# The last output tile of a fused attention and FFN kernel, computed and stored in two column halves

## Chip, cores and metric

The kernel runs on one core of one Trainium2 chip. The metric is the device time of one execution in microseconds (us); the time given for a kernel is the median over several executions. Engine names in the profile: PE is the matrix engine, PEld its weight loads, DVE the vector engine, ACT the scalar engine, POOL the general engine, SP the engine that mostly issues transfers. A "q" behind a name (SPq, ACTq) marks an instruction that the engine's sequencer issues, such as a DMA.

## What is computed

The reference is dilated sliding-window attention with 8 batches, 8 heads, 576 positions and head size 64, followed by a multiplicative feed-forward network without any non-linearity:

```python
attn = softmax(where(mask, q @ k.T / 8, -1e9))   # per head; half of the heads dilated by 4
x = (attn @ v).transpose(0, 2, 1, 3).reshape(4608, 512)
out = ((x @ w1) * (x @ w2)) @ w3 @ w_out         # d_ff 1024, output 4608 x 512, float32
```

## The kernel before

The kernel fuses `w3 @ w_out` into one matrix `wf_sb` early on, so that the network is two "up" products, an elementwise gate and one "down" product. Attention works batch by batch; its result lies transposed in the tiles XT. The up products (line 553) work on units of 288 tokens and chunks of 128 of the hidden size; ACT copies the first of a pair out of PSUM (564), and DVE multiplies it by the second into the ring `gt` (569). The down product (line 580) takes 128 tokens at a time: eight matmuls, one for each 128 of the hidden size, add up into one PSUM bank of 512 columns. For all tiles but the last, `copy_y` copies the bank to an SBUF tile `osb` on ACT (line 591), and `store` issues the transfer of its rows to memory on SP (line 614), mostly in two DMAs, because the tokens of a residue class lie four rows apart in the output. `osb` has three buffers.

The order of the work is made by a small planner (the class Plan). Each step is given to it with an engine, an assumed duration, what it depends on, a priority and the PSUM banks it needs. The planner plays the steps through in time, always taking the ready step with the smallest priority number, and chooses a bank. The instructions are then emitted in the order of the planned starts, so that each engine has one fixed order. The semaphore waits between engines are put in by the framework from what each instruction reads and writes.

The 36 down steps are added by `downs(i)` (line 929), with rising priority numbers. The last one, i = 35, comes after all up products are done; TensorE then has nothing but the last three down tiles left. Its output is not handled by `copy_y` and `store` but by `finish` (line 594): ACT copies columns 0 to 255 (601), DVE columns 256 to 511 (602), ACT issues the store of the first half (603) and SP that of the second (604). All 128 rows of this tile are one DMA for each half.

Of the kernel before, what the change touches and what calls it, by code (L numbers as in the profile page):

```python
# [10 lines left out]
P = 128  # L11
BF16 = mybir.dt.bfloat16
F32 = mybir.dt.float32
U32 = mybir.dt.uint32
AL = mybir.AluOpType
ACT = mybir.ActivationFunctionType
# [11 lines left out]
RING = 1152  # L28
# [31 lines left out]
class Plan:  # L60
# [10 lines left out]
    def add(self, name, eng, dur, deps, fn, prio, slot=0, lat=150, after=()):  # L71
        t = Task(name, eng, dur, deps, fn, prio + SHIFT.get(name, 0), slot, lat, after)
        self.tasks.append(t)
        return t
# [105 lines left out]
def kernel(  # L180
# [11 lines left out]
    nc = tc.nc  # L192
    B, H, s_, d_ = q.shape
    assert (s_, d_) == (S, D) and H == 8
    d_model = H * D
# [3 lines left out]
    KFF = d_ff // P  # L199
# [8 lines left out]
    wk_pool = ctx.enter_context(tc.tile_pool(name="wk", bufs=2))  # L208
# [7 lines left out]
    wf_sb = const.tile([P, KFF, d_model], BF16, name="wf_sb")  # L216
# [4 lines left out]
    gt = const.tile([P, KFF, RING], BF16, name="gt")  # L221
# [10 lines left out]
    def bank(n, dtype=F32):  # L232
        at = ps[:, plan.now.place or 0, :]
        return (at if dtype == F32 else at.bitcast(dtype))[:, 0:n]
# [306 lines left out]
    held = {}  # L541
# [34 lines left out]
    def down(i):  # L576
        y = bank(d_model)
        c0 = (i * P) % RING
        for f in range(KFF):
            nc.tensor.matmul(  # L580
                out=y,
                lhsT=gt[:, f, c0 : c0 + P],
                rhs=wf_sb[:, f, :],
                start=(f == 0),
                stop=(f == KFF - 1),
            )
        held[("y", i)] = y

    def copy_y(i):
        o_sb = wk_pool.tile([P, d_model], F32, tag="osb", bufs=3, name="osb")  # L590
        nc.scalar.copy(out=o_sb, in_=held[("y", i)])  # L591
        held[("o", i)] = o_sb

    def finish(i):

        o_sb = wk_pool.tile([P, d_model], F32, tag="osb", bufs=3, name="osb")
        b, x = i * P // S, i * P % S
        row = b * S + 4 * (x % RUN) + RES[x // RUN]
        rows = out[row : row + 4 * (P - 1) + 1 : 4, :]
        lo, hi = slice(0, d_model // 2), slice(d_model // 2, d_model)  # L600
        nc.scalar.copy(out=o_sb[:, lo], in_=held[("y", i)][:, lo])
        nc.vector.tensor_copy(out=o_sb[:, hi], in_=held[("y", i)][:, hi])
        nc.scalar.dma_start(out=rows[:, lo], in_=o_sb[:, lo])
        nc.sync.dma_start(out=rows[:, hi], in_=o_sb[:, hi])

    def store(i):
        o_sb = held[("o", i)]
        c0, end = i * P, (i + 1) * P
        at = c0
        while at < end:  # L610
            n = min(end, (at // RUN + 1) * RUN) - at
            b, x = at // S, at % S
            row = b * S + 4 * (x % RUN) + RES[x // RUN]
            nc.sync.dma_start(
                out=out[row : row + 4 * (n - 1) + 1 : 4, :], in_=o_sb[at - c0 : at - c0 + n, :]
            )
            at += n
# [9 lines left out]
    def w3_keep(ft):  # L627
        w3T[ft] = wk_pool.tile([P, KFF, P], BF16, tag="w3T", bufs=3, name="w3T")
        nc.scalar.copy(out=w3T[ft], in_=held[("x3", ft)])  # L629
# [21 lines left out]
    add = plan.add  # L651
# [29 lines left out]
    c0 = add("const2", "DVE", 1400, [c1], constants, -98)  # L681
# [39 lines left out]
    for i, nm in enumerate(WHOLE):  # L721
        t = add(f"LF{nm}", "SP", 100, [], lambda nm=nm: load_whole(nm, rows_of[nm], 0), -9 + i,
                lat=4400 + 1350 * i)
# [29 lines left out]
    FUSED, w3m = [], []  # L753
    for ft in sorted(lw3):
        x = add(f"W3T{ft}", "PE", 450, [lw3[ft], idt], lambda f=ft: w3_back(f), RANK["W"], slot=1,
                after=w3m[-3:-2])
        y = add("W3C", "ACT", 1012, [x], lambda f=ft: w3_keep(f), RANK["C"], lat=100, after=w3m[-3:-2])
# [5 lines left out]
        name = f"W3D{ft}"  # L763
# [30 lines left out]
    for b in range(B):  # L794
# [9 lines left out]
        for u in range(2):  # L804
# [3 lines left out]
            for half in range(2):  # L808
# [5 lines left out]
                name = f"VK{b}.{u}.{half}"  # L814
# [5 lines left out]
        if b >= DIRECT_V:  # L820
            hal = add(f"HALO{b}", "DVE", 820, LV[b] + [c0], lambda b=b: halo_v(b), 10 * b + 2,
                      lat=80)
# [46 lines left out]
        while steps < 4 * B:  # L869
            bb, i = steps // 4, steps % 4  # L870
# [7 lines left out]
            n = f"{bb}.{i}"  # L878
# [5 lines left out]
            if (bb, i) == (0, 2) and LATE:  # L884
                for t in late:
# [3 lines left out]
                     after=[prev["x"][i]])  # L889
# [5 lines left out]
            if bb < TURNED:  # L895
                x = add("X" + n, "PE", 310, ns + [idt], st.back, bb - 99 + rank("X", bb), slot=1)
                name = f"K{n}"
# [9 lines left out]
    seq = 10  # L907
    G, Y, gates, stores, pairs = {}, {}, [], [], []
# [20 lines left out]
    def downs(i):  # L929
        nonlocal seq  # L930
        seq += 1
        ks = {i * P // UNIT, (i * P + P - 1) // UNIT}
        y = add(f"Y{i}", "PE", 1728, [G[(k, f)] for k in ks for f in range(KFF)] + FUSED,
                lambda: down(i), seq, slot=1)
        Y[i] = y
        if i == n_y - 1:
            add("FIN", "ACT", 400, [y], lambda: finish(i), -1, lat=100, after=stores[-3:-2])
            return
        cy = add("CY", "ACT", 585, [y], lambda: copy_y(i), -1, lat=100,
                 after=[stores[-3] if len(stores) > 2 else None])  # L940
        stores.append(add("ST", "SP", 300, [cy], lambda: store(i), 0, lat=3000))

    n_y = n_tok // P
    done = 0
    half = KFF // 2
    begin = [(k, f + h) for h in (0, half) for k in range(2) for f in range(half)]
    for k, f in begin + [(k, f) for k in range(2, 2 * B) for f in range(KFF)]:
        ups(k, f)
        if k > 1 and f % 3 == 1 and (done + 1) * P <= k * UNIT:
            downs(done)  # L950
            done += 1
    while done < n_y:
        downs(done)
        done += 1
# [42 lines left out]
```

## Time and profile before

| | |
|---|---|
| median of 6 runs | 256.37 us (256.05 to 256.83) |
| profiled execution, its own time | 256.36 us |
| its span, first to last instruction | 254.6 us |
| granted TensorE clock, mean | 0.999 |
| HBM read, written | 38.80 MB, 9.44 MB |
| down matmuls L580, one | 379 ns |
| weight load for one (L580 PEld) | 98 ns |
| ACT copy of a whole tile (L591) | 586 ns |
| store on SP (L614), issue to landing, min/median/max | 1.6/2.6/7.8 us |

The span runs from the first to the last instruction that the hardware profiler recorded. A chain row gives a start, a length, the engine, the tile written and the source line; in the timeline, what stands in brackets is how long the engine was idle before the instruction and who released it. Matmuls are pipelined: the duration of one is a latency, and the distance between starts says how fast they go. A DMA's row is its issue only; its landing is a time of its own.

### The profile page before, as it was taken

Reading aid. Unit: us, or ns where it says so; the run is one execution under the profiler, and the core shown is the slowest. Engines: PE = TensorE matmul, PEld = TensorE weight load, DVE = VectorE, ACT = ScalarE, POOL = GpSimd, SP = SyncE. Lnnn points to the kernel's source line nnn. Section 1 sums busy time; section 2 is a strip of 40 time slices with the busy share of each in tenths; the row PEclk is TensorE's granted clock in tenths of the full one; section 3 lists DMA queues with packets and bytes.
Section 4 is the critical chain, followed back from the end, with each engine's and each line's share of the span. In section 5 each row is a group of like instructions: output and inputs, shape, how many; then the busy total and the mean of one; then the engine's idle time right before and its main releaser. Section 6 shows DMA issues by size and latency. Waiting matters only on the chain.

```text
span 254.6 us, 6758 instructions
## 1 busy us (share of the span) xinstructions
PE 244.5 (96%) x2723; PEld 169.3 (66%) x2755; DVE 165.3 (65%) x341; ACT 126.2 (50%) x221; POOL 66.4 (26%) x103
## 2 busy tenths in 40 slices
PE   7699999999999999999999999999999999999993
PEld 3488766565767666667676766676767667777661
DVE  3983447799889888678767877837737365333220
ACT  5677333986635534462626526355353543333331
POOL 7643129543522703008260310700000000000000
PEclk9999999999999999999999999999999999999999
DMA  7999999999999999829999667852232222311113
GB/s 225 208 199 206 206 211 211 207 99 181 189 146 182 206 187 170 185 67 147 162 162 144 89 78 103 136 84 64 67 65 67 66 68 73 99 41 44 41 41 124
DMA packets 59230, 33.40 MB, mean 131 GB/s; under 512 B 44736, under 2 KB 49088, under 8 KB 59200
## 3 DMA queue, kind: packets, MB, share of 16 engines
q0 software_dynamic: 38544, 18.81, 57.7%
q1 hardware_dynamic: 20512, 14.03, 24.2%
q8 instruction: 21, 0.34, 0.6%
q10 hardware_dynamic: 144, 0.13, 0.2%
q14 instruction: 9, 0.07, 0.1%
HBM read 38.80 MB, written 9.44 MB: 189 GB/s over the span
## 4 chain that ended last, share of the span: by engine, by line
PE 92%; ACT 3%; DMA 2%; DVE 1%; issue 1%; ACTq 0%
PE ps L553 50%; PE ps L580 24%; PE ps L634 5%; PE ps L481 4%; PE ps L445 4%; DMA gt<-in_q_dram 2%; ACT et L456 2%; PE ps L676 2%; PE ps L622 1%; PE ps L403 1%; PE ps L521 1%; ACT w3T L629 1%; DVE qt L394 1%; ACT qn L271 0%; DVE kt L379 0%
## 5 line engine op out<-in xcount | busy, mean ns | idle before, releaser
L553 PE MATMUL ps<-XT,w_sb 128*128 128x288 bf16 x1024 | 136.2, 286 | 0.0
L553 PEld LDWEIGHTS <-w_sb 128*128 128x128 bf16 x1024 | 97.8, 98 | 30.6
L569 DVE TENSOR_TENSOR gt<-ps,asb 128x288 bf16<-128x288 f32 x128 | 57.7, 455 | 52.0 <-PE ps L553 49.6
L564 ACT CAST asb<-ps 128x288 bf16<-128x288 f32 x128 | 50.9, 399 | 51.8 <-PE ps L553 49.5
L580 PE MATMUL ps<-wf_sb,gt 128*128 128x512 bf16 x260 | 65.9, 379 | 1.5
L591 ACT COPY osb<-ps 128x512 f32<-128x512 f32 x35 | 20.5, 586 | 56.3 <-PE ps L580 56.3
L580 PEld LDWEIGHTS <-gt 128*128 128x128 bf16 x288 | 28.2, 98 | 27.8
L293 POOL DMA_DIRECT2D vp<-in_v_dram x48 | 29.9, 630 | 43.1 <-PE ps L481 18.5
L456 ACT ACTIVATE et<-ps 128x1920 bf16<-128x1920 f32 (+2 forms) x21 | 34.2, 1634 | 5.5 <-PE ps L445 4.9
L504 DVE TENSOR_TENSOR xo<-ps,rcp 96x384 bf16<-96x384 f32 (+1 forms) x48 | 31.5, 675 | 0.6
L464 DVE TENSOR_TENSOR et<-et,mask 128x960 bf16<-128x960 bf16 (+1 forms) x34 | 21.4, 646 | 4.9 <-ACT et L456 4.7
L394 DVE STREAM_TRANSPOSE qt<-qn 128x320 uint32<-128x320 uint32 (+3 forms) x34 | 22.4, 669 | 2.1 <-ACT qn L271 1.9
L481 PEld LDWEIGHTS <-et 128*128 128x128 bf16 x384 | 14.3, 98 | 1.7
L481 PE MATMUL ps<-vp,et 128*128 128x65 bf16 x384 | 15.1, 193 | 0.0
L634 PE MATMUL ps<-wo_sb,w3T 128*128 128x512 bf16 x60 | 14.4, 379 | 0.4
L394 DVE STREAM_TRANSPOSE kt<-kn 128x320 uint32<-128x320 uint32 (+3 forms) x18 | 11.6, 642 | 4.4 <-PE ps L445 4.3
L445 PE MATMUL ps<-qt,kt 32*128 32x96 bf16 x768 | 12.1, 201 | 1.8 <-DVE kt L379 1.8
L445 PEld LDWEIGHTS <-kt 32*128 32x128 bf16 x768 | 9.1, 92 | 6.9 <-issue 4.5
L492 DVE RECIPROCAL rcp<-ps 96x12 f32<-96x12 f32 x32 | 6.8, 216 | 10.4 <-PE ps L481 10.1
L245 POOL DMA_DIRECT2D kn<-in_k_dram x8 | 5.5, 685 | 25.6 <-DVE kt L394 14.9
L379 DVE STREAM_TRANSPOSE kt<-kn 128x576 uint32<-128x576 uint32 (+1 forms) x9 | 9.9, 1121 | 1.4 <-PE ps L445 1.4
L634 PEld LDWEIGHTS <-w3T 128*128 128x128 bf16 x64 | 5.9, 98 | 6.8 <-ACT w3T L629 0.6
(53 smaller groups left out, 114.6 us busy)
## 6 DMA issues: line engine op xcount, KB each, us to landing
qn<-in_q_dram POOLq DMA_DIRECT2D x7, 576.0 KB, 8.3
kn<-in_k_dram POOLq DMA_DIRECT2D x7, 576.0 KB, 7.8
w3n<-in_moe_w_dram POOLq DMA_DIRECT2D x8, 256.0 KB, 14.9
out_dram<-osb SPq DMA_DIRECT2D x7, 256.0 KB, 2.5
out_dram<-osb SPq DMA_DIRECT2D x8, 224.0 KB, 2.8
vp<-in_v_dram POOLq DMA_DIRECT2D x6, 288.0 KB, 10.2
out_dram<-osb SPq DMA_DIRECT2D x8, 192.0 KB, 3.0
out_dram<-osb SPq DMA_DIRECT2D x8, 160.0 KB, 3.8
```

The lines of the kernel that those rows point to most:

```text
L293: nc.gpsimd.dma_start(out=vp[32 + p0 : 32 + p0 + n, 4:8, m, 0:D], in_=v_rows(b, 4, 4 * t0 + res, [[4 * D, n], [S * D, 4], [1, D]]),)
L394: nc.vector.transpose(out=o, in_=i)
L445: nc.tensor.matmul(out=self.sp[:, g, QB * i : QB * i + QB], lhsT=kt[prt, u, QB * m : QB * m + P, c], rhs=qq, start=(c == 0 and not biased) ...
L456: nc.scalar.activation(out=ev, in_=self.sp[:, :, 0:x], func=ACT.Exp, scale=scale)
L464: nc.vector.tensor_tensor(out=ev, in0=ev, in1=mk, op=AL.mult)
L481: nc.tensor.matmul(out=self.o[:, g, mm, :], lhsT=grp.et[:, c0 : c0 + P], rhs=vps[self.b % 2][:, 4 * self.u + g, 3 * self.hf + mm, 0 : D + ...
L504: nc.vector.tensor_tensor(out=dst, in0=self.o[0:QB, hs, :, 0:D], in1=self.rcp[0:QB, hs, :].unsqueeze(3).to_broadcast([QB, n, 3, D]), op=AL ...
L553: nc.tensor.matmul(out=o, lhsT=w_sb[:, c, f * P : (f + 1) * P], rhs=unit_cols(k, c), start=(j == 0), stop=(j == DCH - 1),)
L564: nc.scalar.copy(out=a_sb, in_=held[("a", k, f)])
L569: nc.vector.tensor_tensor(out=gt[:, f, c0 : c0 + UNIT].rearrange("p (r m t) -> p m r t", r=2, m=BLK), in0=held[("b", k, f)].rearrange("p ( ...
L580: nc.tensor.matmul(out=y, lhsT=gt[:, f, c0 : c0 + P], rhs=wf_sb[:, f, :], start=(f == 0), stop=(f == KFF - 1),)
L634: nc.tensor.matmul(out=o, lhsT=w3T[ft][:, g, :], rhs=wo_sb[:, g, :], start=(g == 0), stop=(g == KFF - 1),)
```

## The change

Only the last tile is handled differently. Its eight matmuls of 512 columns become two groups of eight with 256 columns each, each group in a PSUM bank of its own (`down_part`). `finish` is called once for each half. For the first half, DVE copies 256 columns and SP stores them. For the second, DVE copies its first 128 columns and SP stores them, then ACT copies the remaining 128 columns and issues their store. All four share one `osb` tile. In the planner the one down step of 1728 ns becomes two of 880 ns, and the one finishing step on ACT becomes two on DVE.

```diff
+    def down_part(i, half):
+        y = bank(d_model // 2)
+        c0 = (i * P) % RING
+        for f in range(KFF):
+            nc.tensor.matmul(
+                out=y,
+                lhsT=gt[:, f, c0 : c0 + P],
+                rhs=wf_sb[:, f, half * d_model // 2 : (half + 1) * d_model // 2],
+                start=(f == 0),
+                stop=(f == KFF - 1),
+            )
+        held[("y", i, half)] = y
+
-    def finish(i):
-
-        o_sb = wk_pool.tile([P, d_model], F32, tag="osb", bufs=3, name="osb")
+    def finish(i, half):
+
+        if half == 0:
+            held[("o", i)] = wk_pool.tile([P, d_model], F32, tag="osb", bufs=3, name="osb")
+        o_sb = held[("o", i)]
...
-        lo, hi = slice(0, d_model // 2), slice(d_model // 2, d_model)
-        nc.scalar.copy(out=o_sb[:, lo], in_=held[("y", i)][:, lo])
-        nc.vector.tensor_copy(out=o_sb[:, hi], in_=held[("y", i)][:, hi])
-        nc.scalar.dma_start(out=rows[:, lo], in_=o_sb[:, lo])
-        nc.sync.dma_start(out=rows[:, hi], in_=o_sb[:, hi])
+        c0, n = half * d_model // 2, d_model // 2 if half == 0 else d_model // 4
+        nc.vector.tensor_copy(out=o_sb[:, c0 : c0 + n], in_=held[("y", i, half)][:, 0:n])
+        nc.sync.dma_start(out=rows[:, c0 : c0 + n], in_=o_sb[:, c0 : c0 + n])
+        if half == 1:
+            nc.scalar.copy(out=o_sb[:, c0 + n :], in_=held[("y", i, half)][:, n:])
+            nc.scalar.dma_start(out=rows[:, c0 + n :], in_=o_sb[:, c0 + n :])
...
-        y = add(f"Y{i}", "PE", 1728, [G[(k, f)] for k in ks for f in range(KFF)] + FUSED,
-                lambda: down(i), seq, slot=1)
+        need = [G[(k, f)] for k in ks for f in range(KFF)] + FUSED
+        if i == n_y - 1:
+            for half in range(2):
+                y = add(f"Y{i}{'ab'[half]}", "PE", 880, need, lambda h=half: down_part(i, h),
+                        seq + half, slot=1)
+                add("FIN", "DVE", 300, [y], lambda h=half: finish(i, h), half, lat=100,
+                    after=stores[-3:-2])
+            return
+        y = add(f"Y{i}", "PE", 1728, need, lambda: down(i), seq, slot=1)
         Y[i] = y
-        if i == n_y - 1:
-            add("FIN", "ACT", 400, [y], lambda: finish(i), -1, lat=100, after=stores[-3:-2])
-            return
```

## The prediction

> **What bounds the kernel now.** I read the page's first two parts, then the chain of work that ended last for the final stretch, then the timeline and the DMA view of the same stretch.
>
> ```profile
> PE 244.5 (96%) x2723; PEld 169.3 (66%) x2755; DVE 165.3 (65%) x341; ACT 126.2 (50%) x221; POOL 66.4 (26%) x103
> PE   7699999999999999999999999999999999999993
> PEclk9999999999999999999999999999999999999999
> PE 92%; ACT 3%; DMA 2%; DVE 1%; issue 1%; ACTq 0%
> ```
>
> TensorE is busy for 244.5 of 254.6 us at a full granted clock, and it carries 92% of the chain. The change touches nothing before the last output tile, so all of its effect lies in the last slice, where the PE digit falls to 3. The chain of the last stretch (start, us, what):
>
> ```profile
> 245.19 5.14 PE ps L580 x23
> 250.33 0.03 ACTq L601
> 250.35 0.04 issue
> 250.39 0.38 ACT osb L601
> 250.78 0.02 issue
> 250.80 0.42 DVE osb L602
> ```
>
> Nothing but L580 matmuls runs up to 250.33; then the two copies come one after the other. The timeline of the same stretch adds the issues:
>
> ```profile
> 249.28 0.79 SPq L614 DMA_DIRECT2D out_dram<-osb  x2
> 250.39 0.37 ACT L601 COPY osb<-ps 128x256 f32<-128x256 f32 x1 [1.14 <-PE ps L580]
> 250.80 0.37 ACTq L603 DMA_DIRECT2D out_dram<-osb  x1
> 250.80 0.42 DVE L602 COPY osb<-ps 128x256 f32<-128x256 f32 x1 [5.10 <-ACT osb L601]
> 251.25 0.35 SPq L604 DMA_DIRECT2D out_dram<-osb  x1
> ```
>
> The two copies are on two engines, yet DVE waits for ACT. The last store is issued at 251.25; in the trace it lands at 253.33, and the span ends at 254.55. So the tail is 4.22 us from the last matmul: 0.92 to the last issue, 2.08 from issue to landing, 1.22 of closing. Only the first two can be shortened here. The profiled execution took 256.36 us for a span of 254.6, so about 1.8 lies outside the span and stays; it equals the median of 256.37, so I subtract from 256.36.
>
> **The change, part by part.**
>
> *Matmuls.* Eight matmuls of 512 columns become sixteen of 256, with eight more weight loads. The timeline shows a whole tile at 240.30 taking 1.89 us; chain pieces of the inner matmuls give 216 ns each (1.73 for 8), and one matmul lasts 379 ns. The row with 256 columns is the filler at L676:
>
> ```profile
> 16.26 1.64 PE ps L676 x15
> L676 PE MATMUL ps<-warm 128*128 128x256 bf16 x37 | 4.9, 272 | 0.0
> ```
>
> That is 109 ns from one to the next, each with its own weight load, and 272 ns for one. The last tile starts at 250.33 - 1.89 = 248.44. The first half ends at 248.44 + 7 x 0.109 + 0.272 = 249.48, the second at 248.44 + 15 x 0.109 + 0.272 = 250.35: a loss of 0.02 us.
>
> A rule of the Trainium skill speaks against this step: "TensorE: Matmul & The Clock Gate", in the section "The mechanism", says that a weight load overlaps matmuls in flight only when it goes to another row group. All loads here fill all rows. By the rule each matmul would pay its load, 98 ns in the L580 weight row: 16 x (109 + 98) = 3.31 us, not 16 x 109 = 1.74, and the end would come 1.6 us later. The rows decide: L676 and L580 are both full-array, and at 109 and 216 ns they leave no room for 98 ns more. I take nothing for it.
>
> *First half's copy and store.* DVE copies 256 columns in 0.42 us (the L602 row) from about 249.53 to 249.96, under the second half's matmuls, which last to 250.35. Its store goes to SP, whose L614 issues for the tile before end at 250.07; with the usual gap of some 0.05 between SP's issues it runs from 250.14 to 250.49. Both cost nothing, covered by TensorE; without that cover they would cost 0.42 + 0.35. Queued behind the copy on DVE is only the second half's copy, ready at 250.41, and behind the store on SP only the next store, ready at 250.73. SP's issues usually take 0.31 to 0.42, but one of the 63 took 1.28; such a slip could reach the next store.
>
> *Second half.* What was "ACT 256, then DVE 256" becomes "DVE 128, then ACT 128". DVE starts at 250.35 + 0.06 = 250.41. No row shows a DVE PSUM copy of 128 columns. The nearest are L602 (256 columns, 424 ns) and L647 (512, 689 ns): 1.035 ns a column, so 424 - 132 = 292 ns; a 12-column reciprocal from PSUM (L492) at 216 ns and the 424 bound it. DVE ends at 250.70, and SP issues its store at 250.73. For ACT, 373 ns at 256 columns and 586 at 512 give 0.83 ns a column, so 267 ns at 128 (373 bounds it above; L350's 227 ns for 48 columns below).
>
> Does ACT wait for DVE, as DVE waited for ACT? In the trace the wait at L602 can be of two kinds: both copies read one PSUM bank, and both write one tile, osb. "PSUM — Partial Sum Buffer", in the section "PSUM bank collisions raise a hardware error", says that two engines reading one bank in the same partitions at once collide, whichever columns they read, and must be kept apart by a semaphore. By that rule the wait is the bank's, the second half's two copies are again in series, and the first half, in a bank of its own, is free of both. By the other reading the whole osb tile is guarded, and then the first half's store stands in the way too (a rival below). The trace alone doesn't name the cause. I take the bank: ACT runs from 250.73 to 251.00, and its store is issued at 251.03, against 251.25 now: 0.22 us earlier.
>
> *Issue to landing.* In the trace, L603's 128 KB on the ACT queue took 2.03 us: 0.87 from issue to the first packet, 0.54 of packets, 0.62 from the last packet to landing. Half the bytes in the same 128 rows would need 0.27 by bytes or still 0.54 by packets, so 1.76 to 2.03. L614's quickest landing was 1.6, so shorter is possible. The packets are nearest to moving by bytes (2048-byte ones took 84 ns, 1024-byte ones 46). The older store is still in the way: the packets of the two L614 stores end at 251.24, the first half's then need 0.53 (to 251.77), SP's quarter 0.27 (to 252.04), while ACT's may start at 251.03 + 0.87 = 251.90 and share the engines for 0.14. So they end at 251.90 + 0.27 + 0.14 = 252.31 and land at 252.93, against 253.33: 0.40 us earlier (bounds: 251.03 + 2.03 = 253.06 and 251.03 + 1.76 = 252.79, gains of 0.27 and 0.54).
>
> *Closing.* After the last landing SP still goes through five waits for older stores, at 0.06 us each, in the order of the store semaphores. One more store puts one less behind the last: 0.06 gained if that order holds, otherwise nothing.
>
> *What else moves.* One more issue on SP, priced above; the plan's order before the last tile is as before, because the two new down steps have TensorE's last priority numbers and only the two finishing steps depend on them. One more PSUM bank is needed at the end, when the gates are through with theirs. The second half's matmuls could wait for a bank's last reader: the one latest done is L591's copy, which ends at 249.26, before the second half begins at 249.31.
>
> Sum: 0.40 + 0.06 = 0.46, the matmuls' 0.02 being already in the starts. 256.36 - 0.46 = 255.90 us. Of 256.37 that is 0.18%, while 0.2% (0.51 us) is about what a measurement of this kernel can tell from no change.
>
> **The rivals.**
>
> *The forecast, chance 0.70:* 255.75 to 256.1 by the bounds above (gains of 0.27 to 0.60); half a tenth more for the spread of the runs.
>
> *A landing that doesn't shrink and no wait saved in the closing, 0.14:* the L614 stores speak for it: 32 and 64 KB land after 2.1 and 2.0 us near the end, no sooner than 128 KB (though most of these wait behind another on their queue). Then only 0.22 is left, or 0.1 with a slower DVE copy: 256.1 to 256.25.
>
> *The two quarter copies run together, 0.05:* if the wait at L602 had another cause than the bank or the tile, ACT copies from 250.41 to 250.68 and issues at 250.71, 0.32 sooner than forecast: about 255.6. The 5.10 us that DVE sat before L602 speaks against it.
>
> *Slower, 0.09:* the second DVE copy writes osb while SP's store of the first half reads it. If the whole tile is guarded, DVE waits for that landing: packets to 251.77 and 0.65 more is 252.42. Then DVE to 252.74, ACT to 253.04, issue at 253.07, landing at 254.83 to 255.10: later than now by 1.5 to 1.8, so about 257.9. It makes the kernel slower as soon as the second copy starts 0.46 us late. Against it stand the gates: the L569 gate at 240.57 writes gt columns while the L580 matmuls from 240.30 to 242.19 read others of gt, and it doesn't wait, so parts of an SBUF tile are told apart there.
>
> *Slower by weight loads, 0.02:* as worked out above, about 257.5.
>
> **How the numbers follow.** Below 255.85 (faster by over 0.2%) lie a little under half of the forecast and the parallel copies: 0.70 x 0.46 + 0.05 = 0.37. Above 256.88 lie the two slower cases, 0.11. The rest, 0.52, is within 0.2%. The range from 255.55 to 256.35 holds the forecast and the small gain with the runs' spread, and leaves out the slower cases, most of the parallel case's lower half and some of the tails.
>
> **What the profile after should show.** Sixteen matmuls of 272 ns in the last tile, ending near 250.35; a DVE copy of 256 columns before that end; a 128-column DVE copy near 0.29 starting at once after the last matmul, not at 252.4; an ACT copy of 0.27 behind it; a last issue near 251.03; landing after about 1.9. I am wrong if the second DVE copy is late, if the issue is later than 251.25, or if the landing still takes 2.1 with the closing unchanged.

## The result, and the profile after

The changed kernel takes 255.82 us (median of 18 runs, 255.69 to 256.59), against 256.38 for the kernel before (38 runs): 0.56 us less. The ratio is 0.9975, 95% interval 0.9969 to 0.9982. The forecast was 255.90, 0.46 us below the profiled 256.36.

The page of the changed kernel, to be set beside the one of before:

```profile
PE 245.2 (96%) x2731; PEld 170.1 (67%) x2763; DVE 165.6 (65%) x342; ACT 126.1 (50%) x221; POOL 66.4 (26%) x103
PE   7799999999999999999999999999999999999994
PEclk9999999999999999999999999999999999999999
```

There are eight matmuls and eight weight loads more in the records, one DVE copy more, and the clock is as it was. Up to the last tile the two traces agree to 0.07 us (its matmuls start at 248.42 before, at 248.49 after). The chain of work that ended last (start, us, what; "issue" is time in which the engine waited for nothing that the profile shows):

```profile
245.25 3.40 PE ps L580 x15
248.65 1.76 PE ps L598 x16
250.41 0.02 issue
250.44 0.30 DVE osb L616
250.74 0.03 ACTq L619
250.77 0.04 issue
250.81 0.27 ACT osb L619
```

Two copies in series end it, as before, but they hold 128 columns each: the piece from 250.44 to 251.08 is 0.64 us, where before it was 0.83. The timeline shows what has moved ahead:

```profile
248.49 1.91 PE L598 MATMUL ps<-wf_sb,gt 128*128 128x256 bf16 x16
249.56 0.42 DVE L616 COPY osb<-ps 128x256 f32<-128x256 f32 x1 [3.80 <-DMA out_dram<-osb]
250.22 0.88 SPq L617 DMA_DIRECT2D out_dram<-osb  x2
250.44 0.29 DVE L616 COPY osb<-ps 128x128 f32<-128x128 f32 x1 [0.45 <-PE ps L598]
250.81 0.27 ACT L619 COPY osb<-ps 128x128 f32<-128x128 f32 x1 [1.49 <-DVE osb L616]
251.10 0.37 ACTq L620 DMA_DIRECT2D out_dram<-osb  x1
```

The first DVE copy lies wholly under the matmuls. The second starts 0.04 after the last of them, which ends at 250.40. ACT follows DVE. In brackets, "3.80 <-DMA" names an older store, but that one landed only at 249.76, after the copy had begun. The first half's last matmul ended at 249.52, 0.04 before the copy; it is what came last, and e8's row of the same copy (below) names it. The DMA view from 249 us on has the landings (KB, us from issue):

```profile
out_dram<-osb SPq DMA_DIRECT2D x1, 64.0 KB, 1.9
out_dram<-osb ACTq DMA_DIRECT2D x1, 64.0 KB, 1.8
```

From the last matmul's end in the trace (250.31 before, 250.40 after) to the end of the span, the tail divides so:

| us | before | after | difference |
|---|---|---|---|
| last matmul to last store's issue | 0.94 | 0.70 | -0.24 |
| issue to landing of that store | 2.08 | 1.76 | -0.32 |
| landing to the span's end | 1.22 | 1.22 | 0 |
| sum | 4.24 | 3.68 | -0.56 |

The matmuls end 0.08 later in this execution: 0.02 is the sixteen shorter ones, the rest had come about before the last tile. So the spans of these two executions differ by 0.47.

### The profile page after: what moved, and what is told of

The parts are those of the page before. It is cut to its first block, busy times and chain, and to the rows that moved or that the text cites. A ratio compares the mean times of both kernels' runs of the same rounds, so it can differ in the third digit from the quotient of the medians.

```text
span 254.1 us, 6777 instructions
## 1 busy us (share of the span) xinstructions
PE 245.2 (96%) x2731; PEld 170.1 (67%) x2763; DVE 165.6 (65%) x342; ACT 126.1 (50%) x221; POOL 66.4 (26%) x103
## 4 chain that ended last, share of the span: by engine, by line
PE 92%; ACT 3%; DMA 2%; DVE 1%; issue 1%; ACTq 0%
PE ps L553 50%; PE ps L580 23%; PE ps L650 5%; PE ps L481 4%; PE ps L445 4%; DMA gt<-in_q_dram 2%; ACT et L456 2%; PE ps L692 2%; PE ps L638 1%; PE ps L403 1%; PE ps L521 1%; ACT w3T L645 1%; PE ps L598 1%; DVE qt L394 1%; ACT qn L271 0%
## 5 line engine op out<-in xcount | busy, mean ns | idle before, releaser
L580 PE MATMUL ps<-wf_sb,gt 128*128 128x512 bf16 x252 | 64.2, 379 | 1.5
L580 PEld LDWEIGHTS <-gt 128*128 128x128 bf16 x280 | 27.4, 98 | 26.9
```

The source lines that it names most:

```text
L580: nc.tensor.matmul(out=y, lhsT=gt[:, f, c0 : c0 + P], rhs=wf_sb[:, f, :], start=(f == 0), stop=(f == KFF - 1),)
```

## The experiments

The times are medians. Beside each experiment, on the same chip, the kernel before took 256.35 us (e1 to e7) or 256.36 (from e8 on). A ratio's interval is wide where single runs lie far above the median; a conclusion is drawn only where the median and the trace say the same.

**e1: the second half whole.** Does the split into quarters over two engines bring the gain?

```diff
-        c0, n = half * d_model // 2, d_model // 2 if half == 0 else d_model // 4
-        nc.vector.tensor_copy(out=o_sb[:, c0 : c0 + n], in_=held[("y", i, half)][:, 0:n])
-        nc.sync.dma_start(out=rows[:, c0 : c0 + n], in_=o_sb[:, c0 : c0 + n])
-        if half == 1:
-            nc.scalar.copy(out=o_sb[:, c0 + n :], in_=held[("y", i, half)][:, n:])
-            nc.scalar.dma_start(out=rows[:, c0 + n :], in_=o_sb[:, c0 + n :])
+        c0, n = half * d_model // 2, d_model // 2
+        if half == 0:
+            nc.vector.tensor_copy(out=o_sb[:, c0 : c0 + n], in_=held[("y", i, half)][:, 0:n])
+            nc.sync.dma_start(out=rows[:, c0 : c0 + n], in_=o_sb[:, c0 : c0 + n])
+        else:
+            nc.scalar.copy(out=o_sb[:, c0 : c0 + n], in_=held[("y", i, half)][:, 0:n])
+            nc.scalar.dma_start(out=rows[:, c0 : c0 + n], in_=o_sb[:, c0 : c0 + n])
...
-                add("FIN", "DVE", 300, [y], lambda h=half: finish(i, h), half, lat=100,
+                add("FIN", ("DVE", "ACT")[half], 300, [y], lambda h=half: finish(i, h), half, lat=100,
```

> The two matmul halves stay; the second half is copied whole by ACT (256 columns) and stored whole on ACT's queue, so the split into quarters over two engines is undone. Theory (the gain comes from the first half's copy and store going ahead under the second half's matmuls; a store lands sooner in proportion to its bytes): ACT copies 0.37 us from 250.46, issues at 250.86, 128 KB land after 2.03, at 252.89 against 252.87 in the changed kernel: 255.85 us, the same as the changed kernel. Rival 1 (the gain is the quarter split over two engines and queues): most of the gain is lost, 256.2 to 256.4. Rival 2 (a landing of 1.76 does not depend on the bytes but on the emptier engines): landing at 252.62, 255.55 us.

255.82 us (255.74 to 259.33, 7 runs; ratio 0.9994, 0.9961 to 1.0027). The interval, drawn out by one run, decides nothing; the median and the trace do. Timeline of e1:

```profile
250.15 0.39 SPq L618 DMA_DIRECT2D out_dram<-osb  x1
250.41 0.37 ACT L620 COPY osb<-ps 128x256 f32<-128x256 f32 x1 [1.16 <-PE ps L598]
250.81 0.37 ACTq L621 DMA_DIRECT2D out_dram<-osb  x1
```

and its row of the DMA view:

```profile
out_dram<-osb ACTq DMA_DIRECT2D x1, 128.0 KB, 2.0
```

The store is issued 0.48 after the last matmul instead of 0.70, and takes 1.99 to land instead of 1.76. Both kernels land 2.47 after the last matmul. The quarters save 0.22 of landing and pay 0.22 for the second copy in series: here the split over two engines and queues is worth nothing, and both rivals fall.

**e2: one matmul group, the changed copies.** The other half of the change alone.

```diff
-            for half in range(2):
-                y = add(f"Y{i}{'ab'[half]}", "PE", 880, need, lambda h=half: down_part(i, h),
-                        seq + half, slot=1)
+            y = add(f"Y{i}", "PE", 1728, need, lambda: down(i), seq, slot=1)
+            for half in range(2):
...
-        nc.vector.tensor_copy(out=o_sb[:, c0 : c0 + n], in_=held[("y", i, half)][:, 0:n])
+        nc.vector.tensor_copy(out=o_sb[:, c0 : c0 + n], in_=held[("y", i)][:, c0 : c0 + n])
...
```

> One group of eight 512-column matmuls as before, but the copies and stores of the changed kernel (DVE 256 and SP, DVE 128 and SP, ACT 128 and ACT's queue), all after the last matmul and from one PSUM bank. Theory: the three copies are in series, 0.42 + 0.29 + 0.27 with hand-overs, so ACT issues at about 251.5, and 64 KB land after 1.76, at 253.3: 256.3 us, no gain over before (256.38) and at most 0.1 below. Rival (three smaller stores over two queues are what helps): 255.9 to 256.0.

256.24 us (256.10 to 258.18, 14 runs; ratio 0.9997, 0.9983 to 1.001). Timeline of e2:

```profile
250.31 0.62 DVE L616 COPY osb<-ps 128x256 f32<-128x256 f32 x2 [4.65 <-PE ps L580]
251.08 0.27 ACT L619 COPY osb<-ps 128x128 f32<-128x128 f32 x1 [1.87 <-DVE osb L616]
251.38 0.37 ACTq L620 DMA_DIRECT2D out_dram<-osb  x1
```

Without the early half nothing is hidden: the last landing is 2.99 after the last matmul (3.02 before, by the recorded ends). So the gain needs the two matmul groups. The median is 0.11 below the kernel before; of that, 0.03 is this landing and 0.06 the closing (1.16 instead of 1.22, see e8).

**e3: what does ACT wait for?** ACT's quarter gets an SBUF tile of its own; the PSUM bank stays shared.

```diff
-            nc.scalar.copy(out=o_sb[:, c0 + n :], in_=held[("y", i, half)][:, n:])
-            nc.scalar.dma_start(out=rows[:, c0 + n :], in_=o_sb[:, c0 + n :])
+            o_q = wk_pool.tile([P, d_model], F32, tag="osb", bufs=3, name="osb")[:, 0 : d_model // 4]
+            nc.scalar.copy(out=o_q, in_=held[("y", i, half)][:, n:])
+            nc.scalar.dma_start(out=rows[:, c0 + n :], in_=o_q)
```

> The changed kernel, but ACT's quarter goes to an SBUF tile of its own; the two quarters still lie in one PSUM bank. If the wait of ACT for DVE comes from the shared bank: ACT still starts after the DVE copy, 255.8 us as the changed kernel. If it comes from the shared osb tile: ACT copies from 250.46 beside DVE, issues at 250.76 instead of 251.10, and the kernel takes 255.5 us.

255.85 us (255.76 to 256.88, 9 runs; ratio 0.9985, 0.9974 to 0.9996). Timeline of e3:

```profile
250.42 0.29 DVE L616 COPY osb<-ps 128x128 f32<-128x128 f32 x1 [0.45 <-PE ps L598]
250.78 0.27 ACT L620 COPY osb<-ps 128x128 f32<-128x128 f32 x1 [1.49 <-DVE osb L616]
```

The wait is still there with nothing shared but the bank, of which the two copies read different columns. The buffer that ACT's copy writes had been free since 249.90, when its last store landed, so it isn't what ACT waits for. It is the bank.

**e4: a bank for each piece.** Three matmul groups of 256, 128 and 128 columns, one osb tile; DVE and SP take the first two pieces, ACT and its queue the third.

```diff
+    CUTS = (0, 256, 384, 512)
...
+        lo, hi = CUTS[half : half + 2]
+        y = bank(hi - lo)
...
+            for half in range(3):
...
+                add("FIN", ("DVE", "DVE", "ACT")[half], 300, [y], lambda h=half: finish(i, h), half, lat=100,
```

> Three groups of matmuls (256, 128, 128 columns), each in a PSUM bank of its own; DVE copies the first two and SP stores them, ACT copies the third and stores it on its queue; one osb tile. If the bank is what keeps the last two copies apart: ACT copies right after the last matmul, from 250.46, and issues at 250.76, 0.34 earlier than the changed kernel; packets are then near the rate of the 16 engines (about 524 KB from 250.16 at 300 GB/s: not before 251.9), so landing at 252.5 to 252.65: 255.5 to 255.65 us. If the shared osb tile makes ACT wait for DVE's copy or SP's store, ACT starts later and the time is 255.8 or above. Rival on the matmuls (24 weight loads and 128 columns no longer hide one behind the other): the last matmul ends 0.4 later and the gain is gone.

255.87 us (255.78 to 256.14, 10 runs; ratio 0.9976, 0.9966 to 0.9986): a miss. Timeline of e4:

```profile
249.52 0.74 DVE L620 COPY osb<-ps 128x256 f32<-128x256 f32 x2 [3.80 <-DMA out_dram<-osb]
250.18 0.88 SPq L621 DMA_DIRECT2D out_dram<-osb  x2
250.46 0.27 ACT L623 COPY osb<-ps 128x128 f32<-128x128 f32 x1 [1.18 <-PE ps L601]
250.75 0.37 ACTq L624 DMA_DIRECT2D out_dram<-osb  x1
```

and its DMA view:

```profile
out_dram<-osb ACTq DMA_DIRECT2D x1, 64.0 KB, 2.1
```

Both DVE copies lie under the matmuls (DVE ends at 250.26, the last matmul at 250.37), ACT waits for TensorE and no longer for DVE, and the issue is 0.35 earlier. But the store lands at 252.88, when the changed kernel's did (252.87), after 2.13 instead of 1.76. The expectation's bound on the packets was too good: the 524 KB took from 250.12 to 252.25, which is 246 GB/s and not 300. As DVE was through 0.2 before ACT started, this run doesn't show whether ACT would have waited for it with only the osb tile in common.

**e5: e4 without the older store.** Is it the 256 KB of the tile before? Its store is left out, so 128 rows of the output are not written.

```diff
-                    after=stores[-3:-2])
+                    after=stores[-2:-1])
...
+        if i == n_y - 2:
+            return
         stores.append(add("ST", "SP", 300, [cy], lambda: store(i), 0, lat=3000))
```

> Three groups as in e4, but the store of the tile before the last (256 KB) is left out, so that tile's rows of the output are not written. In e4 the last store was issued 0.35 earlier than in the changed kernel and landed at the same time, after 2.13 instead of 1.76. If the older store's packets in the 16 engines held it back: the last store now lands after 1.7 to 1.8 from 250.75, at 252.5, 255.5 us. If something else makes a store issued so soon land late (the receipt, or two issues on two queues at once): 255.85 us as in e4.

255.50 us (255.41 to 255.87, 6 runs; ratio 0.9963, 0.9949 to 0.9977). SP's row of e5's timeline, and the same row of its DMA view:

```profile
249.93 0.83 SPq L621 DMA_DIRECT2D out_dram<-osb  x2
out_dram<-osb ACTq DMA_DIRECT2D x1, 64.0 KB, 1.7
```

The issue is 0.38 after the last matmul as in e4, the landing after 1.71: in e4 the older store had held the last one back by 0.42 (0.14 of it before the first packet, 0.12 in the packets, 0.16 behind the last). It did so at least in part through what was queued behind it. In e4 its own packets end at 251.26 and the last store's begin at 251.78, among those of SP's two stores of the last tile; with the older store gone, these two are issued 0.20 and 0.24 sooner, counted from the last matmul.

**e6 and e7: the older store made early instead.** The tile before the last is computed in halves too. DVE copies its first half and SP stores it, ACT copies the second and stores it on its queue; e6 with e4's last tile, e7 with that of the changed kernel.

```diff
+        if i == n_y - 2:
+            for half in range(2):
+                y = add(f"Y{i}{'ab'[half]}", "PE", 880, need, lambda h=half: half_34(i, h),
+                        seq + 0.1 * half, slot=1)
+                z = add("FH", ("DVE", "ACT")[half], 350, [y], lambda h=half: finish_34(i, h), -1,
+                        lat=100, after=old)
...
+            (nc.sync, nc.scalar)[half].dma_start(
+                out=out[row : row + 4 * (n - 1) + 1 : 4, cols], in_=o_sb[at - c0 : at - c0 + n, cols]
```

> e4, and the tile before the last is also computed in two halves: DVE copies its first half and SP stores it, ACT copies the second and stores it on its own queue. Its 256 KB can then start some 0.4 to 0.9 earlier. If the older store's packets are what held e4 back: last landing at 252.5 to 252.6, 255.5 to 255.6 us, less than both kernels. If the six smaller stores cost more on the queues (two issues of 0.4 on ACT ahead of its last copy, 0.4 more on SP) than they give: 255.85 or above.

> The changed kernel, with the tile before the last in two halves as in e6. If the changed kernel is now bound by the chain of its two quarter copies (last issue at 251.10, landing after 1.76, near the 1.6 to 1.7 of a store alone), the older store matters little: 255.75 to 255.85 us. If its packets matter as much as in e4: 255.5 us.

e6: 255.35 us (255.26 to 255.91, 5 runs; ratio 0.9959, 0.9942 to 0.9975). Timeline of e6:

```profile
249.02 0.86 ACTq L655 DMA_DIRECT2D out_dram<-osb  x2
250.34 0.27 ACT L623 COPY osb<-ps 128x128 f32<-128x128 f32 x1 [1.35 <-PE ps L601]
250.64 0.36 ACTq L624 DMA_DIRECT2D out_dram<-osb  x1
```

The issues of the older half on ACT's queue end at 249.88, before its last copy. The last store lands after 1.81, 2.14 after the last matmul. e7: 255.72 us (255.56 to 256.13, 9 runs; ratio 0.9970, 0.9958 to 0.9982), its landing 2.48 after the last matmul, as in the changed kernel. Two rows of its timeline:

```profile
250.68 0.27 ACT L619 COPY osb<-ps 128x128 f32<-128x128 f32 x1 [1.72 <-DVE osb L616]
250.98 0.36 ACTq L620 DMA_DIRECT2D out_dram<-osb  x1
```

So with the quarters in one bank the chain of the two copies binds, and the older store hardly matters; with a bank for each piece the older store binds. For the landing each alone gives nothing (2.50 after the last matmul in e4, 2.48 in e7, 2.47 in the changed kernel), both together 0.33.

**The changed kernel again**, with no edit, on the same chip as e5 to e7:

> The changed kernel itself once more, beside the next three on the same chip: 255.8 to 255.9 us.

255.83 us (255.66 to 259.30, 22 runs; ratio 0.9992, 0.9975 to 1.001). Its trace has the tail of the first one: the landing 2.47 after the last matmul, 1.22 of closing.

**e8 and e9: the order of the closing waits.** e7 was 0.1 below the changed kernel though its landing, counted from the last matmul, was the same. The trace's records of SP's closing waits, each for one store semaphore in a fixed order, show why:

| kernel | waits behind the last landing | landing to the span's end, us |
|---|---|---|
| before, changed, e1, e3, e4 | 5 | 1.22, 1.23 in e3 |
| e2 | 4 | 1.16 |
| e5 | 6 | 1.28 |
| e6, e7 | 2 | 1.03, 1.05 |

Which semaphore a store gets depends on how many stores came before it, and the last two can change places: ACT's store took the earlier one of two in the changed kernel and the later one in e2, which issues the same stores. e8 issues one store of each of the tiles 28 to 31 in two pieces in the changed kernel, e9 those of tiles 29 and 30 in e6:

```diff
+            if i in (28, 29, 30, 31) and n > 63:
+                split.setdefault(i, at)
+                n = n // 2 if split[i] == at else n
```

> The changed kernel, with one store of each of the tiles 28 to 31 issued in two pieces (same rows, same bytes, some 20 us before the end, where SP has room). This moves the semaphores of the last three stores on by four places. In the changed kernel five waits of 0.06 stand behind the last landing in SP's closing list; with this one is left. If the order of the closing waits costs what the prediction took for it: 4 x 0.06 = 0.24 off, 255.6 us. If the closing takes its time whatever the order: 255.83 us as the changed kernel, or a little above for four more issues.

> e6, with two stores more by the same means (tiles 29 and 30), so that the last store's semaphore is the last one in SP's closing list instead of two before it: 2 x 0.06 = 0.12 off e6's 255.35, 255.2 to 255.25 us. If the order costs nothing: 255.35 us.

e8: 255.56 us (255.47 to 256.62, 17 runs; ratio 0.9964, 0.9951 to 0.9978), 0.27 below the changed kernel, with one wait behind the landing and 0.99 of closing. The landing is 2.46 after the last matmul, unchanged, so the gain is the closing's (0.23 of it by the traces). Two rows of its timeline:

```profile
249.48 0.42 DVE L616 COPY osb<-ps 128x256 f32<-128x256 f32 x1 [3.80 <-PE ps L598]
251.02 0.37 ACTq L620 DMA_DIRECT2D out_dram<-osb  x1
```

e9: 255.48 (255.10 to 256.38, 14 runs; ratio 0.9964, 0.9951 to 0.9976), a miss, though its trace has no wait behind the landing and 0.91 of closing. So both were run again, beside each other on one chip:

> e6 once more, so that e6 and e9 stand beside each other on one chip: 255.35 us.

> e9 once more. Its span was 0.07 shorter than e6's and its closing wait list ended 0.11 sooner after the last landing, but its runs spread from 255.1 to 256.4 with a median of 255.48. If that spread was chance: 255.2 to 255.25 us here, 0.1 below e6. If the two extra issues cost what they give: 255.35 to 255.5.

e6: 255.43 us (255.23 to 258.33, 22 runs; ratio 0.9970, 0.9956 to 0.9985); e9: 255.23 (255.11 to 255.95, 6 runs; ratio 0.9964, 0.9952 to 0.9977). The second pair is about as expected, and the traces repeat the first ones: landing 2.14 after the last matmul and 1.03 of closing for e6, 2.13 and 0.93 for e9.

The miss of the first e9 lies outside the span. The median span is 253.5 there and 253.4 in the second pair, against 253.6 in both of e6. But a run's time is not always its span and a fixed rest: for the kernel before, the changed kernel, e1 to e5, e7 and e8 no run took over 1.85 us more than its span, while 10 of the 14 first e9 runs did (up to 2.98) and 9 of the 22 second e6 runs (up to 3.53), and one in each of the other e6 and e9 runs. The two traces of such executions, and no others, have one 16 KB packet of an instruction queue behind the end of the span. For the first e9 it runs from 255.22 to 256.35; the queue's row in the DMA view from 253 us on:

```profile
q8 instruction: 1, 0.02, 1.8%
```

Why it comes there, and only in some runs of e6 and e9, is open. The intervals of e6 and e9 overlap: that e9 beats e6 is shown for the closing in the trace, but not settled for the time. Both are below the kernel before and below the changed kernel's median.

## Why the prediction was right, step by step

- *Matmuls:* right. 272 ns each, 109 ns from one start to the next, sixteen in 1.91 us, no time for the weight loads. The weight-load rival is out. The rule weighed against it (the Trainium skill, "TensorE: Matmul & The Clock Gate", "The mechanism") would have added 1.6 us; the trace decides against the rule here.
- *First half hidden:* right. The copy took 0.42 and ended at 249.99, under matmuls that ended at 250.40; its store was issued at 250.22 (forecast 250.14).
- *Second half's copies:* right. 292 and 266 ns (forecast 292 and 267). The hand-over from DVE to ACT took 0.08 instead of the 0.03 taken; the DVE copy started 0.02 sooner after the last matmul than taken.
- *The cause of the wait:* right. It is the PSUM bank, as the prediction took it from the Trainium skill ("PSUM — Partial Sum Buffer", "PSUM bank collisions raise a hardware error"): e3 keeps the wait, with other columns of the same bank and an SBUF tile of its own. The wait is a semaphore that the framework put in; what the chip does without one, no run here shows. Whether a shared osb tile alone would also make one engine's copy wait for another's isn't tested, as in e4 DVE was through before ACT could start. One reading of the prediction was weak: of the 5.10 us that DVE sat before L602 most is time without work, and only the 0.41 from 250.39, where ACT's copy started, to 250.80 spoke against parallel copies. The slower rival, with the osb tile guarded as a whole, is out: the second DVE copy began at 250.44 while the first half's store was landing (252.52).
- *Issue to landing:* the mechanism right, the term mis-sized. The step "land at 252.93", 1.90 after the issue, measured 1.76. That this is the forecast's lower bound is chance, for the bound was made of other parts (0.27 of packets, 0.62 behind them). The packets took 0.35, from 251.99 to 252.34, instead of the 0.41 allowed for sharing, and the last packet's way to landing 0.53 instead of 0.62. By bytes rather than by packets is confirmed: 1.76 for 64 KB and 1.99 for 128 KB (e1), each in 128 packets of data, which took 27 and 46 ns on average.
- *Closing:* the price right, the place wrong. The step "one more store puts one less behind the last" gave 0.06 and measured 0. ACT's store took the semaphore ahead of SP's second, so five waits stayed behind it. In e2, where it took the later one, four stayed, and the 0.06 came; e8 saves 0.23 with four fewer.

The two misses, -0.14 and +0.06, are what makes the tail 0.56 shorter instead of 0.48. They have opposite signs, so it is luck that the sum came out nearer than the landing alone. The prediction didn't ask what the quarters are worth against a second half stored whole. It had both terms of it, 0.22 of chain and 0.27 of packets, and e1 shows that they cancel (0.22 and 0.22).

## What to carry to other kernels

At a kernel's end, work out for each piece when it is issued and when it lands, and compare splits from that sum: an early half under the last matmuls brought all of the gain here, while a further split in one PSUM bank gave back in series what it saved in bytes. When a copy is made earlier and the landing doesn't move, look at the stores that are still in the engines from the tile before: here two limits stood at the same time, and for the landing only removing both helped. What comes after the last landing isn't fixed either, if it is a list of waits in an order of its own.

## What the runs showed of the hardware

- A store's landing time depended on what another queue was still moving: 64 KB on ACT's queue took 1.71 with the older store left out (e5) and 2.13 with it on SP's queue, which also made SP's next two stores later (e4).
- Two copies in a row on DVE overlap a little: in e2 the 256 and 128 columns took 0.62 together, against 0.42 + 0.29 apart.
- SP's closing list costs 0.06 for each wait, even where the store has landed already (four waits fewer, 0.23 less: e8).
- An execution can end later than its span tells: in two traces an instruction packet of 16 KB runs behind the last instruction, and these executions took 2.71 and 3.53 us more than their span instead of 1.73 to 1.85.
- Matmuls of 128 columns with a weight load each (e4's L601) started 56 ns apart, though one load is recorded at 98 ns.
